# Moving one plane copy ahead of a cast, and two input loads behind two weight loads, in a gated-mix kernel

## The chip, the core and the metric

The kernel runs on one core of a Trainium2 chip. The metric is the device time of one execution in microseconds (us), taken as the median over several runs. The core has five engines that run side by side and wait for each other by semaphores: TensorE (PE, matrix products, with PEld for its weight loads), VectorE (DVE), ScalarE (ACT), GpSimd (POOL) and SyncE (SP, which here only issues DMA transfers). Each engine works through its own instructions in their order.

## The reference

For 2048 tokens of width 512 two branches are computed from one input `x` and mixed by a gate per token:

```
g = sigmoid((x * gate_w).sum(-1))
a = linear attention: q, k, v = x @ wqkv; per head (32 heads of 16)
    phi(t) = [softmax(t @ w_phi), softmax(-t @ w_phi)]
    o = phi_q (phi_k^T v) / (phi_q (phi_k^T 1) + 1e-6);  a = o @ wo
b = experts: q = x @ w_q (32 heads, two halves of 128);
    s1 = q1 @ k1^T, s2 = q2 @ k2^T; the best of 16 in each half names
    one of 256 experts; b = sum over heads of gelu(x . u[e]) * v[e]
out = g * a + (1 - g) * b
```

Two things matter for the change. The scores `s1`, `s2` need products of `w_q` with `k1`, `k2`; the kernel makes these "score weights" once, from 16 pieces `wq0` to `wq15` of 1 MB each, while the attention's keys and values are accumulated. And every token tile of `x` is needed as a pair of a high and a low part.

## The kernel before

The tokens are cut into 16 tiles of 128. A first phase (about the first 120 us) computes keys and values for all tiles, accumulates `phi_k^T v`, and builds the score weights. A second phase runs tile by tile over queries, scores, softmax and output. The order of instructions on every engine is the order in which the program writes them (a manual schedule); only semaphore waits move them in time.

The first phase handles tiles 0 to 4 one by one, and then tiles in pairs (5,6), (7,8), ... in the loop `for t in range(5, NT - 1, 2)`. A pair shares products in a Strassen-like way: `Sums.add` forms sums and differences of the two tiles on POOL, in place in their raw buffers, and `Sums.high` and `Sums.low` split them into high and low parts. The products of a pair are written as PE groups named by their PSUM banks: `pk` (keys), `pe`, `pu`, `pv`.

Loads of `x`: `x_load(t)` gives tile `t` one of four raw buffers (tag `xr`) and issues a 256 KB DMA on SP's queue. `x_high` casts it on ACT (L152), `x_low` subtracts on DVE (L156). In the pass for pair (5,6) the list `more` holds tiles 9 and 10, the second pair behind the one at work.

Score weights: two pieces of `wq` go through PE into one PSUM bank `ws` (`score_w`, L299), and each piece's buffer is then refilled by `load_wq` on SP's queue (L143). Since `ws` comes out in the wrong orientation, it is turned by a DMA transpose on 16-bit planes. `score_planes(j)` copies `ws` to the plane tile `wpl` on ACT (L304) and issues the transpose into `wtp` on SP's queue (L306). A later "join" puts the planes together: `join_tp` copies `wtp` to the f32 tile `wtj` on ACT (L315), and `join_end` casts `wtj` to the high part `sh` on ACT (L321) and subtracts the low part `sl` on POOL (L322). `wpl`, `wtp` and `wtj` have one buffer each, so that a plane copy waits for the transpose before it, a transpose for the join copy before it, and a join copy for the POOL subtraction before it. In the pass t = 5 there are two joins: the one of `ws1` and, after `score_planes(2)` (the score weights made in the pass of tile 4), the one of `ws2`. `score(1)` twice then makes `ws3` and calls `score_planes(3)`.

`k_diffs`, `k_exp`, `k_sum`, `k_mult` are the softmax of one tile's keys: DVE (L115 to L121), ACT (L267), DVE (L271, L272), POOL (L276).

Of the kernel before, what the change touches and what calls it, by code (L numbers as in the profile page):

```python
# [9 lines left out]
F32 = mybir.dt.float32  # L10
# [10 lines left out]
P = 128  # L21
S = 2048
D = 512
NT = S // P
# [11 lines left out]
def mix_kernel(ctx, tc, xT, wqT, wkT, wv, wphi, wo, wq, kk, ug, ev, cst, out):  # L36
# [6 lines left out]
    def mm_bank(name):  # L43
        return psum.tile([P, 512], F32, tag="mm", bufs=4, name=name)

    def tr_bank(name):
        return psum.tile([P, 512], F32, tag="tr", bufs=3, name=name)
# [24 lines left out]
    def x_parts(i, first):  # L72
        xt[i, first] = x_part(i, first)
# [59 lines left out]
    wa_ = ca.enter_context(tc_pool("wl", "left"))  # L133
# [6 lines left out]
    def stage(src, name, shape=None):  # L140
        t_ = wa_.tile(shape or [P, NK, D], F32, tag="st", bufs=2, name=name)
        if src is not None:
            sp.dma_start(t_, src)  # L143
        return t_

    def x_load(t):
        r = rawx[t] = wa_.tile([P, NK, P], F32, tag="xr", bufs=4, name=f"xr{t}")
        if t > 0:
            sp.dma_start(r, xT[t])

    def x_high(t, ks=slice(0, NK)):
        (dve.tensor_copy if t < 3 else act.copy)(x_of(t)[0][:, ks], rawx[t][:, ks])  # L152

    def x_low(t, ks=slice(0, NK)):
        h, l = x_of(t)
        dve.tensor_tensor(l[:, ks], rawx[t][:, ks], h[:, ks], op=ALU.subtract)  # L156

    def x_split(t, ks=slice(0, NK)):
        x_high(t, ks)
        x_low(t, ks)  # L160
# [80 lines left out]
    phis, vs, pks, wsP, stk, joins = {}, {}, {}, {}, {}, []  # L241

    def v_tile(t):
        v = vs[t] = home(t).tile([P, H, F + 1], F32, name=f"v{t}", tag="v")
        if t < NT - 1:
            pool.memset(v[:, :, F], 1.0)
        return v[:, :, :F]
# [9 lines left out]
    def k_diffs(t):  # L257
        phis[t] = home(t).tile([P, 1024], F32, tag="d", name=f"d{t}")
        stk[t] = w1.tile([P, 192], F32, tag="stt", name=f"st{t}")
        softmax_diffs(pks.pop(t), phis[t], stk[t])  # L260
# [5 lines left out]
    def k_exp(t):  # L266
        act.activation(phis[t], phis[t], AF.Exp)  # L267

    def k_sum(t):
        d, st = phis[t], stk[t]  # L270
        dve.tensor_reduce(st[:, 64:128], g64(d), axis=AX.X, op=ALU.add)  # L271
        dve.reciprocal(st[:, 128:192], st[:, 64:128])  # L272

    def k_mult(t):
        d, st = phis[t], stk.pop(t)
        pool.tensor_tensor(g64(d), g64(d), b64(st[:, 128:192]), op=ALU.mult)  # L276

    def kvacc(t):
        n = F + 1 if t < NT - 1 else F
        for g in range(8):  # L280
            for c in range(4):
                h = 4 * g + c
                pe.matmul(acc[32 * c:32 * c + 32, g, :n], phis[t][:, 32 * h:32 * h + 32],
                          vs[t][:, h, :n], start=(t == 0 and g == 0),
                          stop=(t == NT - 1), skip_group_check=True)
# [8 lines left out]
    def score_w(i, raw):  # L294
        j, par = i // 2, i % 2
        if par == 0:
            wsP[j] = tr_bank(f"ws{j}")
        for c in range(4):
            pe.matmul(wsP[j][32 * c:32 * c + 32, :], kp[:, j // 4, par, :], raw[:, c, :],  # L299
                      start=(par == 0), stop=(par == 1))  # L300

    def score_planes(j):
        pl = wa_.tile([P, 2, D], U16, tag="wpl", bufs=1, name=f"wpl{j}")
        act.copy(pl, wsP.pop(j).bitcast(U16).rearrange("p (c j) -> p j c", j=2))  # L304
        tp = wa_.tile([P, 8, P], U16, tag="wtp", bufs=1, name=f"wtp{j}")
        sp.dma_start_transpose(tp, pl.rearrange("p j c -> p (j c)"))  # L306
        joins.append((j, tp))
# [6 lines left out]
    def join_tp(j, tp, tj):  # L314
        act.copy(tj.bitcast(U16).rearrange("p (k n j) -> p j k n", j=2, n=P),  # L315
                 tp.rearrange("p (j k) n -> p j k n", j=2))

    def join_end(j, tj):
        js = slice(P * j, P * j + P)
        t3 = tj.rearrange("p (k e) -> p k e", k=NK)  # L320
        act.copy(sh[:, :, js], t3)  # L321
        pool.tensor_tensor(sl[:, :, js], t3, sh[:, :, js], op=ALU.subtract)  # L322
# [56 lines left out]
    def load_wq():  # L379
        if len(raws) < 16:  # L380
            raws.append(stage(wq[len(raws)], f"wq{len(raws)}"))
# [11 lines left out]
    def spare(src, name, shape):  # L393
        t_ = wa_.tile(shape, F32, tag="xr", bufs=4, name=name)
        sp.dma_start(t_, src)
        return t_
# [3 lines left out]
    def score(n, planes=True):  # L400
        nonlocal done
        for _ in range(n):
            score_w(done, raws[done])
            done += 1
            load_wq()
            if planes and done % 2 == 0:
                score_planes(done // 2 - 1)

    def join_all():
        old = list(joins)  # L410
        joins.clear()
        for j, tp in old:
            score_join(j, tp)
# [39 lines left out]
    def prod(o, left, right, first):  # L453
        for i, ((ah, al), (bh, bl)) in enumerate(zip(left, right)):
            for j, (x_, w_) in enumerate(((ah, bh), (ah, bl), (al, bh))):
                pe.matmul(o, x_, w_, start=(first and i + j == 0), stop=(i == 1 and j == 2),  # L456
                          skip_group_check=True)
# [8 lines left out]
    for t in range(5, NT - 1, 2):  # L466
        n = t + 1
        more = [u for u in (t + 4, t + 5) if u < NT]
        for u in more:
            x_load(u)  # L470
        if t == NT - 5:
            rawu = [spare(ug[:, 0:2], "rawu0", [P, 2, NU])]
        elif t == NT - 3:
            rawu.append(spare(ug[:, 2:4], "rawu1", [P, 2, NU]))
            rawe = [spare(ev[:, 0], "rawe0", [P, D])]
        for u in (t + 2, t + 3):
            if u < NT - 1:
                x_low(u)
        if behind:
            k_diffs(behind)  # L480
        a = pks[t] = mm_bank(f"pk{t}")
        prod(a, tile_of(t, 0), b11, True)
        b = mm_bank(f"pu{t}")
        act.copy(b, a)
        if t + 3 < NT:
            Sums.add(t + 2)
        if t < NT - 3:
            join_all()
        else:
            (j6, tp), = joins  # L490
            joins.clear()
            tj6 = wa_.tile([P, D], F32, tag="wtj", bufs=1, name="wtj6")
            join_tp(j6, tp, tj6)
        e = tr_bank(f"pe{t}")
        prod(e, sums(0, 2), b1, True)
        prod(b, sums(1, 0), b2, False)
        c = mm_bank(f"pv{t}")
        act.copy(c, b)
        if t == 5:
            score_planes(2)  # L500
            k_exp(4)
            k_sum(4)
            k_mult(4)
            join_all()
        prod(a, tile_of(t, 2), b21, False)
        k_diffs(t)
        if behind:
            k_exp(behind)
            k_sum(behind)
            k_mult(behind)  # L510
        score(1)
        if t == NT - 3:
            rawq = stage(wqT, "rawq")
        score(1)
        for u in (t - 3, t - 2):
            kvacc(u)
        vn, vt = v_tile(n), v_tile(t)
        act.copy(vn, by16(e))
        k_exp(t)
        k_sum(t)  # L520
        prod(b, sums(0, 0), b3, False)
        d = pks[n] = mm_bank(f"pk{n}")
        act.copy(d, b)
        prod(c, sums(1, 2), b22, False)
        if t == NT - 3:
            x_split(NT - 1)
        dve.tensor_tensor(vt, by16(c), vn, op=ALU.add)
        dve.tensor_tensor(vn, by16(b), vn, op=ALU.add)
        o2 = d.rearrange("p (c n) -> p c n", c=2)
        prod(o2, tile_of(n, 2), b4, False)  # L530
        if t + 3 < NT:
            Sums.high(t + 2)
            Sums.low(t + 2)
        if t == 7:
            for i in range(2):
                x_parts(i, 11)
        for u in more if n < NT - 4 else ():
            x_high(u)
        k_mult(t)
        behind = n  # L540
    t = NT - 1
# [583 lines left out]
```

## Time and profile before

| what | value |
|---|---|
| time, median of 3 runs | 379.39 us (377.92, 379.39, 380.75) |
| time of the profiled execution | 380.27 us |
| its span, first to last instruction | 378.4 us |
| busy: PE, DVE, ACT, POOL | 97%, 88%, 67%, 54% |
| mean granted clock of TensorE | 0.99 |
| DMA read from and written to main memory | 26.43 MB, 4.19 MB |

The profiled execution lies 1.87 us above its own span (380.27 against 378.4): that is work outside the first and last instruction. TensorE is busy nearly everywhere; the few places where it is idle or runs on a reduced clock lie in the first 120 us, which is also where the change is. Shares over the whole span say little about it; the stretch from 47 to 75 us has to be read by itself.

### The profile page before, as it was taken

The numbers are of one execution on the slowest core, as the hardware profiler recorded it, in microseconds if no ns is written. First come the engines' busy times: TensorE is split into PE (matmuls) and PEld (weight loads), VectorE is DVE, ScalarE is ACT, GpSimd is POOL, SyncE is SP. The second block draws the span as 40 slices with busy tenths as digits, with TensorE's granted clock in tenths as the row PEclk, the third lists the DMA queues.
The fourth block names the chain that finished last, engine by engine and source line by source line (L and its number), as shares of the span: only waits on it lengthen the run. The fifth ranks groups of instructions, "written<-read, shape, count | busy, mean of one in ns | idle before, by whom it ended". The sixth has DMA issues, their size and how long they took to land.

```text
span 378.4 us, 8980 instructions
## 1 busy us (share of the span) xinstructions
PE 368.9 (97%) x3519; PEld 289.7 (77%) x3519; DVE 334.0 (88%) x783; ACT 252.6 (67%) x449; POOL 204.4 (54%) x205
## 2 busy tenths in 40 slices
PE   8999996999999999999999999999999999999996
PEld 4766764778668888878878888888888888888775
DVE  4679885898978889999999999999999999999993
ACT  5576656757756444879668677696686686687741
POOL 1189987498658627636427335344454464364700
PEclk9999996999999999999999999999999999999999
DMA  7867796289665031462341452443523523523201
GB/s 277 332 226 238 232 325 201 94 216 269 248 144 126 3 86 57 84 99 69 86 97 46 108 81 63 84 100 31 122 59 68 125 56 72 127 50 78 65 34 55
DMA packets 72218, 46.67 MB, mean 123 GB/s; under 512 B 63600, under 2 KB 64496, under 8 KB 69872
## 3 DMA queue, kind: packets, MB, share of 16 engines
q1 hardware_dynamic: 71312, 45.24, 45.7%
q10 hardware_dynamic: 864, 0.87, 0.8%
q8 instruction: 27, 0.44, 0.5%
q14 instruction: 15, 0.12, 0.1%
HBM read 26.43 MB, written 4.19 MB: 81 GB/s over the span
## 4 chain that ended last, share of the span: by engine, by line
PE 77%; POOL 8%; DMA 5%; ACT 4%; DVE 3%; issue 2%; ACTq 0%; POOLq 0%; DVEq 0%
PE po L850 11%; PE s L56 8%; PE s L57 8%; PE s L58 8%; PE po L857 5%; PE pq L56 5%; PE pq L58 4%; PE pq L57 4%; PE pk L456 3%; PE oT L738 3%; DMA wtp<-wpl 2%; PE pp L57 2%; PE pp L58 2%; PE pp L56 2%; POOL d L276 2%
## 5 line engine op out<-in xcount | busy, mean ns | idle before, releaser
L652 POOL TENSOR_TENSOR w<-d,zb 128x512 f32<-128x512 f32 x32 | 41.1, 1301 | 78.1 <-ACT d L646 78.1
L56 PE MATMUL s<-sh,xh 128*128 128x512 f32 x128 | 50.9, 398 | 0.0
L57 PE MATMUL s<-sl,xh 128*128 128x512 f32 x128 | 49.9, 390 | 0.0
L58 PE MATMUL s<-sh,xl 128*128 128x512 f32 x128 | 49.9, 389 | 0.0
L687 POOL TENSOR_TENSOR d<-d,st 128x512 f32<-128x512 f32 x30 | 31.2, 1061 | 27.8 <-DVE st L681 25.6
L646 ACT ACTIVATE d<-d 128x512 f32<-128x512 f32 x32 | 20.1, 632 | 35.0 <-DVE d L119 26.9
L276 POOL TENSOR_TENSOR d<-d,st 128x1024 f32<-128x1024 f32 x16 | 33.9, 2118 | 16.0 <-ACT d L267 9.2
L729 ACT COPY pt<-tp 128x1024 uint16<-128x1024 uint16 x28 | 36.3, 1366 | 0.0
L719 ACT COPY pl<-d 128x1024 uint16<-128x1024 uint16 x28 | 29.2, 1044 | 6.9 <-POOL d L687 6.9
L58 PEld LDWEIGHTS s<-sh,xl 128*128 128x128 f32 x128 | 24.0, 188 | 5.1
L56 PEld LDWEIGHTS s<-sh,xh 128*128 128x128 f32 x128 | 24.0, 188 | 4.7
L57 PEld LDWEIGHTS s<-sl,xh 128*128 128x128 f32 x128 | 24.1, 188 | 4.6
L271 DVE TENSOR_REDUCE st<-d 128x64 f32<-128x1024 f32 x16 | 19.4, 1213 | 8.5 <-ACT d L267 8.3
L56 PE MATMUL pq<-wah,xh 128*128 128x512 f32 x64 | 26.8, 418 | 0.0
L58 PE MATMUL pq<-wah,xl 128*128 128x512 f32 x64 | 25.1, 392 | 0.0
L57 PE MATMUL pq<-wal,xh 128*128 128x512 f32 x64 | 25.0, 390 | 0.0
L656 DVE TENSOR_REDUCE st<-d 128x32 f32<-128x512 f32 x32 | 21.6, 683 | 1.9 <-ACT d L646 0.4
L696 DVE TENSOR_TENSOR eq<-s,mx 128x512 bf16<-128x512 f32 x32 | 22.1, 692 | 1.2
L156 DVE TENSOR_TENSOR xl<-xr,xh 128x512 fp32r<-128x512 f32 (+2 forms) x17 | 20.7, 1240 | 1.7 <-ACT xh L152 1.6
L695 DVE TENSOR_REDUCE mx<-s 128x32 f32<-128x512 f32 x32 | 21.8, 681 | 0.0
L666 DVE TENSOR_REDUCE st<-w 128x32 f32<-128x512 f32 x32 | 20.4, 676 | 0.1
L267 ACT ACTIVATE d<-d 128x1024 f32<-128x1024 f32 x16 | 17.0, 1064 | 3.9 <-DVE d L121 3.9
(253 smaller groups left out, 1121.9 us busy)
## 6 DMA issues: line engine op xcount, KB each, us to landing
wq<-wq SPq DMA_DIRECT2D x16, 1024.0 KB, 5.7
xr<-xT SPq DMA_DIRECT2D x15, 256.0 KB, 5.1
y<-ot SPq DMA_DIRECT2D x15, 256.0 KB, 2.4
rawk<-wkT SPq DMA_DIRECT2D x1, 1024.0 KB, 6.3
rawq<-wqT SPq DMA_DIRECT2D x1, 1024.0 KB, 6.4
rawo<-wo SPq DMA_DIRECT2D x4, 256.0 KB, 3.7
rawu<-ug SPq DMA_DIRECT2D x2, 258.0 KB, 3.2
rawv<-wv ACTq DMA_DIRECT2D x2, 256.0 KB, 4.4
```

Source lines behind the costliest of these rows:

```text
L56: pe.matmul(o, ah, bh, start=(first and i == 0), stop=False)
L57: pe.matmul(o, ah, bl, start=False, stop=False)
L58: pe.matmul(o, al, bh, start=False, stop=(last and i == n - 1))
L276: pool.tensor_tensor(g64(d), g64(d), b64(st[:, 128:192]), op=ALU.mult)
L652: pool.tensor_tensor(hs(e["w"], i), hs(e["ph"], i), hs(zb, i), op=ALU.mult)
L656: dve.tensor_reduce(pair(e["st"][:, 64:128])[:, :, i], hs(e["ph"], i), axis=AX.X, op=ALU.add)
L687: eng.tensor_tensor(g64(d)[:, gs_], g64(d)[:, gs_], r[:, gs_].unsqueeze(2).to_broadcast([P, 32, F]), op=ALU.mult)
L695: dve.tensor_reduce(mx, p3, axis=AX.X, op=ALU.max)
L696: dve.tensor_tensor(e["eq"][:, 512 * half:512 * half + 512].rearrange("p (h f) -> p h f", f=F), p3, mx.unsqueeze(2).to_broadcast([P, H, F] ...
L719: act.copy(pl, e["ph"][:, halves[i]].bitcast(U16).rearrange("p (c j) -> p j c", j=2))
L729: act.copy(p16[:, :, 4 * i:4 * i + 4, :], e["tp"][i].rearrange("p (j g) n -> p j g n", j=2))
L850: pe.matmul(po, a, b, start=(i == 0), stop=False)
```

## The change

In the pass t = 5 alone, `score_planes(2)` moves forward. Instead of standing behind the join of `ws1` and the copy of `pv5`, its plane copy stands between that join's two halves, directly behind `join_tp`. And in the same pass the loads of `x` tiles 9 and 10 no longer open the pass; they are issued after the second `score(1)`, behind the refills `wq8`, `wq9` and the transpose of `ws3`. No instruction is added or removed: ACT keeps 433 rows, SP 128, PE 2058, DVE 735 and POOL 177 in the listing, and on PE, DVE and POOL their order is the same.

```
@@ -466,8 +466,9 @@
     for t in range(5, NT - 1, 2):
         n = t + 1
         more = [u for u in (t + 4, t + 5) if u < NT]
-        for u in more:
-            x_load(u)
+        if t > 5:
+            for u in more:
+                x_load(u)
@@ -484,7 +485,14 @@
-        if t < NT - 3:
+        if t == 5:
+            (j1, tp), = joins
+            joins.clear()
+            tj1 = wa_.tile([P, D], F32, tag="wtj", bufs=1, name="wtj1")
+            join_tp(j1, tp, tj1)
+            score_planes(2)
+            join_end(j1, tj1)
+        elif t < NT - 3:
             join_all()
@@ -497,7 +505,6 @@
         if t == 5:
-            score_planes(2)
             k_exp(4)
@@ -512,6 +519,9 @@
         score(1)
+        if t == 5:
+            for u in more:
+                x_load(u)
         for u in (t - 3, t - 2):
             kvacc(u)
```

ACT in the first half of the pass t = 5. The names are tiles with the tile or join number and a buffer number behind it. Before:

```order
L484 COPY pu5_590<-pk5_583 128x512
L315 COPY wtj1_596<-wtp1_453 128x2x512
L321 CAST sh_71<-wtj1_596 128x4x128
L498 COPY pv5_613<-pu5_590 128x512
L304 COPY wpl2_615<-ws2_532 128x1024
L267 ACTIVATE d4_526<-d4_526 128x1024
L315 COPY wtj2_623<-wtp2_617 128x2x512
```

Now:

```order
L485 COPY pu5_586<-pk5_579 128x512
L315 COPY wtj1_592<-wtp1_453 128x2x512
L304 COPY wpl2_594<-ws2_532 128x1024
L321 CAST sh_71<-wtj1_592 128x4x128
L506 COPY pv5_613<-pu5_586 128x512
L267 ACTIVATE d4_526<-d4_526 128x1024
L315 COPY wtj2_619<-wtp2_596 128x2x512
```

The plane copy `wpl2` has moved up by two instructions; the cast `sh` and the copy `pv5` come one instruction later, and everything from `d4` on keeps its place.

SP's queue over the same pass and the start of the next one. Before:

```order
L143 DMA wq7_543<-wq 128x2048
L149 DMA xr9_577<-xT 128x512
L149 DMA xr10_579<-xT 128x512
L306 DMA_TRANSPOSE wtp2_617<-wpl2_615 128x8x128
L143 DMA wq8_644<-wq 128x2048
L143 DMA wq9_650<-wq 128x2048
L306 DMA_TRANSPOSE wtp3_654<-wpl3_652 128x8x128
L149 DMA xr11_757<-xT 128x512
L149 DMA xr12_759<-xT 128x512
```

Now:

```order
L143 DMA wq7_543<-wq 128x2048
L306 DMA_TRANSPOSE wtp2_596<-wpl2_594 128x8x128
L143 DMA wq8_640<-wq 128x2048
L143 DMA wq9_646<-wq 128x2048
L306 DMA_TRANSPOSE wtp3_650<-wpl3_648 128x8x128
L149 DMA xr9_652<-xT 128x512
L149 DMA xr10_654<-xT 128x512
L149 DMA xr11_757<-xT 128x512
L149 DMA xr12_759<-xT 128x512
```

The two loads `xr9` and `xr10` have moved past two transposes and two 1 MB refills, and now stand directly ahead of `xr11` and `xr12`.

## The prediction

> **What bounds the kernel now.** I read the clock row of the page first, then the chain that ended last, then the stretch from 47 to 75 us engine by engine, and last how long each transfer of that stretch took to land. The change touches only ACT and SP, so ACT's rows come first (start, duration, what; in brackets the idle time before, and its releaser):
>
> ```profile
> 47.34 1.36 ACT L315 COPY wtj<-wtp 128x1024 uint16<-128x1024 uint16 x1
> 48.73 0.62 ACT L321 CAST sh<-wtj 128x512 fp32r<-128x512 f32 x1
> 49.58 0.57 ACT L498 COPY pv<-pu 128x512 f32<-128x512 f32 x1 [0.22 <-PE pu L456]
> 50.06 1.02 ACT L304 COPY wpl<-ws 128x1024 uint16<-128x1024 uint16 x1
> 50.96 1.07 ACT L267 ACTIVATE d<-d 128x1024 f32<-128x1024 f32 x1
> 56.02 1.35 ACT L315 COPY wtj<-wtp 128x1024 uint16<-128x1024 uint16 x1 [3.99 <-POOL sl L322]
> 60.27 0.60 ACT L523 COPY pk<-pu 128x512 f32<-128x512 f32 x1
> 61.82 1.14 ACT L152 CAST xh<-xr 128x512 fp32r<-128x512 f32 x2
> 66.44 0.57 ACT L484 COPY pu<-pk 128x512 f32<-128x512 f32 x1 [3.48 <-PE pk L456]
> ```
>
> ACT stands still for 3.99 us, from 52.03 to 56.02, ahead of the second join copy. From there it works without a gap to the copy `pk` that ends at 60.87, and PE waits for exactly that copy:
>
> ```profile
> 52.70 1.07 PE L299 MATMUL ws<-wq,kp 128*32 128x512 f32 x8 [0.81 <-DMA wq<-wq]
> 57.45 0.39 PE L456 MATMUL pv<-wbh,xl 128*128 128x512 f32 x1
> 60.92 0.79 PE L456 MATMUL pk<-sh,xh 128*128 128x512 f32 x1 [3.08 <-ACT pk L523]
> 67.97 0.39 PE L456 MATMUL pu<-uh,xh 128*128 128x512 f32 x1
> ```
>
> PE loses 3.08 us there, and then more, because the granted clock falls (columns behind the stretch and its length: PE, PEld, DVE, ACT, POOL, clock, DMA share, GB/s):
>
> ```profile
> 57.60:57.90 0.30, 0.24 (x2) 0.00 (x0) 0.00 (x0) 0.30 (x1) 0.29 (x1) 1.00 1.04 437
> 60.00:60.30 0.30, 0.00 (x0) 0.00 (x0) 0.00 (x0) 0.30 (x2) 0.00 (x0) 0.77 0.35 84
> 66.90:67.20 0.30, 0.30 (x2) 0.23 (x2) 0.30 (x2) 0.30 (x2) 0.21 (x1) 0.85 0.00 0
> ```
>
> The clock is 1.00 until about 60.1, 0.50 after that, and full again from about 66.95. The chain gives the price:
>
> ```profile
> 60.92 5.49 PE pk L456 x12
> 66.41 1.72 PE pe L456 x6
> 69.50 1.36 PE pk L456 x6
> 73.81 9.03 DMA wtp<-wpl
> ```
>
> Six such products take 1.36 us at full clock. The twelve at 60.92 took 5.49 instead of 2.72, the next six 1.72 instead of 1.36: 3.1 us lost. So this place costs about 6.2 us in all, 3.1 of idle PE and 3.1 of slow PE. The question is whether the change moves what ends ACT's 3.99 us.
>
> The copy `wtj2` needs two things: the transpose `wtp2`, and the one `wtj` buffer, which POOL's subtraction `sl` of the first join has to leave. POOL and SP (a transfer's row is its issue):
>
> ```profile
> 51.59 0.73 POOL L175 TENSOR_TENSOR xr<-xr 128x256 f32<-128x256 f32 x1 [1.41 <-DVE xl L156]
> 54.70 1.29 POOL L322 TENSOR_TENSOR sl<-wtj,sh 128x512 fp32r<-128x512 f32 x1
> 48.21 1.37 SPq L149 DMA_DIRECT2D xr<-xT  x2
> 51.10 1.24 SPq L306 DMA_TRANSPOSE wtp<-wpl  x1
> wtp<-wpl SPq DMA_TRANSPOSE x1, 3.9
> 58.97 1.24 SPq L306 DMA_TRANSPOSE wtp<-wpl  x1
> 62.81 1.57 SPq L149 DMA_DIRECT2D xr<-xT  x2
> ```
>
> The fifth row is the landing time of the transpose issued at 51.10: it was there at 55.0. POOL's subtraction ended at 55.99, and ACT started 0.03 us later. So POOL sets this wait, and the transpose is 1.0 us early already.
>
> **The change part by part.**
>
> *The plane copy moves up.* It starts where the cast `sh` started, at 48.73, ends near 49.74, and the transpose is issued there instead of at 51.10: 1.4 us earlier. The cast comes about 0.9 us later, near 49.64, and ends near 50.3; its reader, POOL's subtraction, starts at 54.70 behind four sums, so 4.4 us cover it (without them it would cost the 0.9). The copy `pv5` slides from 49.58 to about 50.15, and its products on PE come after 56. The exponential `d4` starts about 0.3 us earlier, since the 0.22 of waiting for `pu` is now filled with work; DVE's sum of `d4` and POOL's product gain nothing from it, because POOL is at its sums and the subtraction until 55.99.
>
> *What the early transpose brings.* Behind `wq7` alone it cannot land later than the 55.0 of before, because `xr9` and `xr10` no longer stand ahead of it and nothing new does. Its earliest by the quickest transpose of the trace (the 3.5 below) is 53.2. Either way `wtj2` still waits for POOL's subtraction. That one stands behind the sums of tiles 7 and 8, which waited for DVE's `xl` (1.41 us idle, first row), and none of these has moved. ACT starts at 56.02 as before: gain 0.0. Bounds: 0, or 1.4 less if the subtraction was not what held ACT.
>
> *The loads of tiles 9 and 10 move down.* They leave SP's queue at 48.21 and come behind the transpose `wtp3`, whose plane copy ACT makes after `wtj2`, unchanged at 57.93 to 58.94. So they are issued after 58.97 plus 1.24, at 60.21 and near 60.55, 12 us later. `wq7` no longer shares the engines with them. Its landing of before:
>
> ```profile
> wq<-wq SPq DMA_DIRECT2D x1, 1024.0 KB, 7.9
> ```
>
> PE waited 0.81 us for it at 52.70. At most that is saved, and it ends in a longer wait of PE for ACT (3.08 becomes up to 3.9), worth 0.0 by itself.
>
> When do the two loads land? The first two rows are loads on quiet engines (issued at 62.81 and next), the third one beside a waiting transpose, the fourth one behind a `wq`; then the transpose itself, quickest and slowest:
>
> ```profile
> xr<-xT SPq DMA_DIRECT2D x1, 256.0 KB, 2.3
> xr<-xT SPq DMA_DIRECT2D x1, 256.0 KB, 2.7
> xr<-xT SPq DMA_DIRECT2D x1, 256.0 KB, 4.8
> xr<-xT SPq DMA_DIRECT2D x1, 256.0 KB, 5.4
> wtp<-wpl SPq DMA_TRANSPOSE x1, 3.5
> wtp<-wpl SPq DMA_TRANSPOSE x1, 9.0
> ```
>
> By 60.2 the `wq` pieces have drained and only `wtp3` is in flight (58.97 plus 3.5, so 62.5), so I take 3.0 to 3.6: tile 9 near 63.3, tile 10 near 64.1; bounds 62.5 (2.3) and 66.0 (5.4). ACT wants tile 9 at 61.82 and stalls about 1.5 us. Behind the two casts it has nothing until 66.44, when PE releases it: the casts then end near 64.8, 1.6 us ahead. With 5.4 they end at 66.6, and `pu` (L484) comes 0.2 us late; PE reads that copy at 67.97, 0.96 us after it was ready at 67.01. So all of it is covered: 0.0. The transpose `wtp3` itself has no new traffic ahead of it.
>
> DVE is the other reader:
>
> ```profile
> 63.48 3.43 DVE L156 TENSOR_TENSOR xl<-xr,xh 128x512 fp32r<-128x512 f32 x2
> L156 DVE TENSOR_TENSOR xl<-xr,xh x2: 1091/1756/2420, 63.5 to 64.5; 128x512 fp32r<-128x512 f32 x2
> 63.97 2.40 POOL L276 TENSOR_TENSOR d<-d,st 128x1024 f32<-128x1024 f32 x1
> 70.96 0.69 DVE L115 TENSOR_REDUCE st<-pk 128x32 f32<-128x512 f32 x1 [1.66 <-PE pk L456]
> 75.31 1.95 POOL L276 TENSOR_TENSOR d<-d,st 128x1024 f32<-128x1024 f32 x1 [3.89 <-ACT d L267]
> ```
>
> The second of the pair took 2.42 us and ended at 66.91, half a microsecond after POOL's product: it was held up by it. If the first now starts near 64 or later, both run after that product, which itself ends a little earlier, and the pair ends at 66.9 to 67.7. DVE's next idle time is 1.66 us, before 70.96, so the up to 0.8 us are covered; uncovered, they would delay the softmax of tile 7 by as much. POOL's sums of tiles 9 and 10 start as much later and have the 3.89 us of idle in the last row behind them.
>
> *The sum.* 0.0 for the transpose, 0.0 for the loads, 0.0 for PE's longer wait: 380.3 us against the profiled execution. That execution lies 0.9 above the median of the runs (379.39), so my time is 379.4.
>
> [...]
>
> **The rivals.**
>
> *The transpose did hold ACT* (faster). The profile calls POOL's spans rough. If the subtraction had ended early and the transpose released ACT, `wtj2` comes up to 1.4 us earlier, PE's idle time falls to 1.7 and the clock may stay up: 1.4 + 3.1 = 4.5 less, 374.9. Against it: a landing 1.0 us before the start, and a start 0.03 us after the subtraction. Chance 0.09.
>
> *The clock stays up* (faster). The runs of before lie 2.83 us apart, close to the 3.1 of the slow stretch, so some may have gone without it. A median without it: 376.3. Against it: PE's idle time does not get shorter. Chance 0.08.
>
> *The clock stays down longer.* PE idles up to 0.8 us more. If the slow stretch of 6.9 us lasts half as long again, 3.4 us at half speed cost 1.7: 381.1. Against it: PE is fully busy from 60.92 on, as before. Chance 0.06.
>
> *The x pair lands late* (slower). From a landing of tile 10 at 66.8, 6.2 us after its issue, ACT's `pu` copy holds up PE. If it took as long as the slowest transpose, 9.0, it lands at 69.6, the copy ends at 70.8 and PE waits 2.8 us; the 3.08 us of before shows that such a gap halves the clock, 3.1 more: 385.3. For it: the loads share the engines with `wtp3`, and ACT, DVE and POOL all stand behind them in order. Against it: no `wq` is ahead of them. Chance 0.11.
>
> **How the numbers follow.** The forecast has 0.66. The range leaves out the first and last rival, 0.20 together: from 376.3 (clock up) to 382.0 (clock down longer, 381.1, and the 0.9 by which an execution can lie above its median). One per cent, about what a measurement of this kernel can tell from no change, is 3.8 us: below 375.6 lies the first rival, above 383.2 the last. Faster 0.09, within 0.80, slower 0.11.
>
> **What would show it.** Right: the transpose is issued near 49.7 and lands by 55; the second `wtj` copy still starts near 56.0, released by POOL `sl` after some 4.3 us; ACT now stalls about 1.5 us before the L152 casts, for the DMA of `xr`; the `pu` copy still waits for PE; PE's gap ahead of `pk` is 3.1 to 3.9 us, with the clock at 0.50 behind it. Wrong: a `wtj2` copy well before 56, a `pu` copy released by the L152 casts, or PE idle near 68.

## The result, and the profile after

In 20 runs of each kernel on the same chip the changed kernel took 379.76 us (378.46 to 381.73), the one before 379.53 (377.50 to 382.24). The ratio is 1.0005, with a 95% interval from 0.9984 to 1.0026: no change that can be measured, as forecast. The profiled execution took 379.06 us, with a span of 377.2. Of the runs further down, one of the twelve executions with the plane copy alone took 514.29 us at a mean clock of 0.656, and the figures of that run leave it out.

In this execution the pass t = 5 begins 0.68 us later than in the one of before (the copy `wtj1` starts at 48.02 instead of 47.34), which lies ahead of everything that the change moves. Times after are to be read with that shift. ACT after the change (start, duration, what; in brackets the idle time before, and its releaser):

```profile
48.02 1.36 ACT L315 COPY wtj<-wtp 128x1024 uint16<-128x1024 uint16 x1
49.24 1.00 ACT L304 COPY wpl<-ws 128x1024 uint16<-128x1024 uint16 x1
50.14 0.63 ACT L321 CAST sh<-wtj 128x512 fp32r<-128x512 f32 x1
51.17 1.06 ACT L267 ACTIVATE d<-d 128x1024 f32<-128x1024 f32 x1
56.72 1.38 ACT L315 COPY wtj<-wtp 128x1024 uint16<-128x1024 uint16 x1 [4.48 <-POOL sl L322]
64.01 1.25 ACT L152 CAST xh<-xr 128x512 fp32r<-128x512 f32 x2 [1.36 <-DMA xr<-xT]
66.28 0.57 ACT L485 COPY pu<-pk 128x512 f32<-128x512 f32 x1 [1.02 <-PE pk L456]
```

The plane copy is the second row now, and the second join copy still starts when POOL's subtraction ends: 56.72, which is 56.02 plus the shift. Its wait grew from 3.99 to 4.48 us, because the work ahead of it ended earlier. The late `x` pair shows as a new wait of 1.36 us before the casts L152; the copy `pu` behind them is still released by PE, 1.02 us after the casts ended. SP's issues and POOL, with the landing time of the first transpose:

```profile
50.27 1.25 SPq L306 DMA_TRANSPOSE wtp<-wpl  x1
wtp<-wpl SPq DMA_TRANSPOSE x1, 4.1
61.02 4.06 SPq L149 DMA_DIRECT2D xr<-xT  x4
52.27 0.73 POOL L175 TENSOR_TENSOR xr<-xr 128x256 f32<-128x256 f32 x1 [1.41 <-DVE xl L156]
55.39 1.29 POOL L322 TENSOR_TENSOR sl<-wtj,sh 128x512 fp32r<-128x512 f32 x1
```

The transpose was issued at 50.27 and was there at 54.4, 2.3 us before the copy that reads it could start: the change bought 1.3 us of a transfer that nobody waited for. PE and DVE:

```profile
53.44 1.06 PE L299 MATMUL ws<-wq,kp 128*32 128x512 f32 x8 [0.87 <-DMA wq<-wq]
61.65 0.50 PE L456 MATMUL pk<-sh,xh 128*128 128x512 f32 x1 [3.04 <-ACT pk L533]
64.66 3.04 DVE L156 TENSOR_TENSOR xl<-xr,xh 128x512 fp32r<-128x512 f32 x2 [0.38 <-ACT xh L152]
70.46 0.69 DVE L115 TENSOR_REDUCE st<-pk 128x32 f32<-128x512 f32 x1 [0.36 <-PE pk L456]
```

PE's gap is 3.04 us, before it was 3.08. DVE's idle time before the keys of tile 7 shrank from 1.66 to 0.36 us. The late pair took little of that: DVE's subtractions for it ended at 67.70, without the shift 0.1 us later than before (67.02 against 66.91). The rest comes from PE, which delivered the keys of tile 7 about 1.2 us sooner (70.46, without the shift 69.78, against 70.96), because its slow stretch was shorter. The only larger difference between the two executions in this stretch is the clock. It fell again, but later and for a shorter time; the twelve products behind the gap took 4.60 us instead of 5.49, and the next six no more than their full-clock time (stretch and length, PE, PEld, DVE, ACT, POOL, clock, DMA share, GB/s; then two rows of the chain):

```profile
61.80:62.10 0.30, 0.30 (x2) 0.26 (x3) 0.30 (x1) 0.30 (x2) 0.00 (x0) 1.00 1.27 226
62.40:62.70 0.30, 0.30 (x2) 0.20 (x2) 0.30 (x1) 0.25 (x1) 0.30 (x1) 0.50 0.65 57
65.70:66.00 0.30, 0.30 (x3) 0.26 (x2) 0.30 (x1) 0.00 (x0) 0.30 (x1) 0.89 0.22 61
61.65 4.60 PE pk L456 x12
66.25 1.38 PE pe L456 x6
```

That is 1.2 us less of slow PE. The two profiled times differ by 1.2 us as well (379.06 against 380.27), but the equal figures are chance. The pass had begun 0.68 us later, so that at the plane copy of `ws4`, in the next pass, 0.5 us of lead was left (72.27 against 72.78), and the transpose that this copy feeds then landed after 7.6 us instead of 9.03:

```profile
72.27 1.01 ACT L304 COPY wpl<-ws 128x1024 uint16<-128x1024 uint16 x1 [1.09 <-PE ws L299]
wtp<-wpl SPq DMA_TRANSPOSE x1, 7.6
80.97 1.38 ACT L315 COPY wtj<-wtp 128x1024 uint16<-128x1024 uint16 x1 [1.33 <-DMA wtp<-wpl]
```

With the plane copy alone the same transpose took at most 10.85 us (issued at 72.65, its join copy started at 83.50), with the loads alone at most 9.41 (72.80 and 82.21). One profile of each kernel can't tie such differences to the change, and over 20 runs the times show none.

### The profile page after: what moved, and what is told of

The parts are those of the page before. It is cut to its first block, busy times and chain, and to the rows that moved or that the text cites. A ratio compares the mean times of both kernels' runs of the same rounds, so it can differ in the third digit from the quotient of the medians.

```text
span 377.2 us, 8980 instructions
## 1 busy us (share of the span) xinstructions
PE 367.1 (97%) x3519; PEld 288.9 (77%) x3519; DVE 332.3 (88%) x783; ACT 253.2 (67%) x449; POOL 204.9 (54%) x205
## 4 chain that ended last, share of the span: by engine, by line
PE 93%; ACT 3%; DMA 1%; DVE 1%; POOL 1%; issue 0%; ACTq 0%; POOLq 0%
PE po L860 11%; PE s L56 8%; PE s L57 8%; PE s L58 8%; PE pk L456 6%; PE po L867 5%; PE pq L56 5%; PE pq L58 4%; PE pq L57 4%; PE ws L299 3%; PE pu L456 3%; PE oT L748 3%; PE kvacc L283 2%; PE pp L57 2%; PE pp L58 2%; PE pp L56 2%
## 5 line engine op out<-in xcount | busy, mean ns | idle before, releaser
L156 DVE TENSOR_TENSOR xl<-xr,xh 128x512 fp32r<-128x512 f32 (+2 forms) x17 | 18.8, 1126 | 1.9 <-ACT xh L152 1.7
```

## The experiments

My theory had three parts: POOL's subtraction holds the second join copy, so the early transpose brings nothing; the late `x` pair is covered; and the gap of PE costs its own length and a slow stretch (3.08 and 3.1 us in the profile of before). The rivals: the transpose did hold ACT; a gain and a loss cancel; the later transposes bound everything anyway. Each ratio is against the kernel before on the same chip: 380.13 us beside the first four runs below, 379.70 beside the last four.

**The two halves of the change, each alone.** The plane copy alone is the changed kernel with the old head of the pass:

```
-        if t > 5:
-            for u in more:
-                x_load(u)
+        for u in more:
+            x_load(u)
...
-        if t == 5:
-            for u in more:
-                x_load(u)
```

> The plane copy moved up, the x loads left where they were. My theory: nothing on the path, 379.5 within 0.5; transpose issued near 49.7 behind the two x loads, second join copy still released by POOL's subtraction. Rival (two effects that cancel: the early copy gains, the late loads lose): 377 to 378.5.

Measured: ratio 0.9984 (0.9958 to 1.0009), 379.89 us. The loads alone are the same edit the other way round, on the kernel before:

> The x loads moved down, the plane copy left where it was. My theory: 379.5 within 0.5; tile 10 lands near 64.5, ACT's casts end before PE releases the next copy. Rival (the late loads cost, hidden in the changed kernel by the gain of the early copy): 380.5 to 382.

Measured: ratio 1.0010 (0.9988 to 1.0033), 380.21 us. Neither half shows an effect by itself. The intervals leave room for a gain of up to 0.4% from the copy and a loss of up to 0.3% from the loads, so that a gain and a loss that cancel would have to be smaller than that; the rows show neither. The second join copy with the plane copy alone, and then with the loads alone, where the casts wait for the pair as well:

```profile
56.09 1.36 ACT L315 COPY wtj<-wtp 128x1024 uint16<-128x1024 uint16 x1 [4.48 <-POOL sl L322]
```

```profile
56.22 1.37 ACT L315 COPY wtj<-wtp 128x1024 uint16<-128x1024 uint16 x1 [3.99 <-POOL sl L322]
64.35 1.26 ACT L152 CAST xh<-xr 128x512 fp32r<-128x512 f32 x2 [2.21 <-DMA xr<-xT]
```

With the loads alone ACT had nothing to spare any more: the copy `pu` followed the casts without idle time, at 65.58. That is one of the prediction's signs of being wrong. It cost PE nothing, since PE read the copy at 66.96, 0.8 us after it was done.

**POOL's sums behind the first subtraction, in the changed kernel.** If POOL holds the copy, then letting the subtraction go first must free it:

```
-        if t + 3 < NT:
+        if t + 3 < NT and t != 5:
             Sums.add(t + 2)
...
             join_end(j1, tj1)
+            Sums.add(t + 2)
```

> The changed kernel, with POOL's four sums of tiles 7 and 8 moved behind the low-part subtraction of the first join, so that the subtraction no longer stands behind them. My theory (POOL's subtraction, not the transpose, ends ACT's wait before the second join copy): the subtraction ends near 52 instead of 56.7, the second join copy starts when the transpose lands, near 54.4 to 54.6, some 2.2 us earlier than in the changed kernel; PE's gap before pk6 falls from 3.0 to about 0.8 us, the clock stays at 1.00, and the whole is 3.5 to 5 us faster than before: 374.5 to 376. Rival A (the transpose held ACT all along, POOL's spans being rough): the copy stays near 56.7 and the time at 379.5. Rival B (the next stage is the bound anyway, the time of the pass is given back at the next transposes): PE's gap closes but the time moves by less than 1 us.

Measured: ratio 0.9992 (0.9962 to 1.0022), 379.80 us. The first half of the expectation came true and the second did not; a time that moves by less than 1 us is what rival B foretold. ACT, POOL and PE:

```profile
54.32 1.37 ACT L315 COPY wtj<-wtp 128x1024 uint16<-128x1024 uint16 x1 [1.23 <-DMA wtp<-wpl]
51.70 1.29 POOL L322 TENSOR_TENSOR sl<-wtj,sh 128x512 fp32r<-128x512 f32 x1 [1.18 <-ACT sh L321]
63.55 1.26 ACT L152 CAST xh<-xr 128x512 fp32r<-128x512 f32 x2 [3.30 <-DMA xr<-xT]
59.23 0.50 PE L456 MATMUL pk<-sh,xh 128*128 128x512 f32 x1 [0.83 <-ACT pk L534]
65.34 0.50 PE L456 MATMUL pu<-uh,xh 128*128 128x512 f32 x1 [1.74 <-ACT pu L485]
70.28 1.01 ACT L304 COPY wpl<-ws 128x1024 uint16<-128x1024 uint16 x1 [1.27 <-PE ws L299]
82.06 1.38 ACT L315 COPY wtj<-wtp 128x1024 uint16<-128x1024 uint16 x1 [4.43 <-DMA wtp<-wpl]
84.63 0.50 PE L456 MATMUL pu<-eh,gh 128*128 128x512 f32 x1 [0.55 <-ACT pv L507]
```

The copy now starts at 54.32, released by the transpose; so it had been POOL. PE's gap fell from 3.04 to 0.83 us, and the clock stayed at 1.00 in this execution. But what stood behind it in the queue came to light: the casts wait 3.30 us for the late pair, and PE 1.74 us for the `pu` copy behind them. I had not counted that the slack which covered the late pair was itself made of PE's gap and its slow clock.

That does not account for the whole loss. At the plane copy of `ws4` this execution was still 2.0 us ahead of the changed kernel's (70.28 against 72.27). The transpose that this copy feeds took 10.66 us, where it had taken 7.6, and the join copy behind it started 1.1 us later than in the changed kernel (82.06 against 80.97); the wait of 0.55 us and another of 0.80 come after it. In this profile the lead was lost at a later transpose, as rival B says. And the clock did not stay up in every run. Five of the twelve had a mean clock of 0.999 or 1.000 and a median of 377.34 us; the other seven, at 0.996 or less, had 380.79. Where it fell in those seven no profile shows.

**The same move in the kernel before** (`Sums.add` behind `join_all()` at t = 5, plane copy and loads where they were):

> The kernel before (late plane copy, x loads ahead), with only POOL's sums moved behind the first join's subtraction. My theory: now the transpose of the second score weights is what ends ACT's wait; it is issued near 51.1 and lands near 55, so the second join copy starts near 55.0: 1.0 us earlier than before, PE's gap 2.1 us, clock uncertain; time 376 to 378.5, that is 1 to 2.5 us slower than the changed kernel with the same move, which is what the early plane copy is worth once POOL is out of the way. Rival (the early plane copy is worth nothing in any case): as fast as the other one, 375.

Measured: ratio 0.9959 (0.9935 to 0.9982), 378.67 us. That is 0.17 us above the expected range, and not slower than the run above, as I had expected it to be: here the pair is early, so that nothing is lost at the casts. The profile shows the copy released by the transpose, after a late issue:

```profile
52.89 1.24 SPq L306 DMA_TRANSPOSE wtp<-wpl  x1
56.56 1.36 ACT L315 COPY wtj<-wtp 128x1024 uint16<-128x1024 uint16 x1 [2.75 <-DMA wtp<-wpl]
```

**Plane copy up, sums behind the subtraction, loads at the head:**

> Plane copy up and POOL's sums behind the first join's subtraction, x loads left at the head of the pass. The run with the late x loads closed PE's gap before pk6 to 0.83 us but then lost 1.74 us at the pu copy, because ACT stood 3.30 us waiting for the x pair. My theory (with the gap closed, the late x pair becomes the next wait): with the loads early ACT has no wait before the x casts, PE's 1.74 us are gone; the transpose is issued near 50.5 and lands near 55, PE's gap is 1 to 2 us and the clock stays up; 376.5 to 378.5, faster than the run with the late loads by 1 to 3 us. Rival (it is the later transposes that bound the stretch after 72 us, whatever the x loads do): 379.5.

Measured: ratio 0.9965 (0.9939 to 0.9990), 379.05 us; 0.55 us above what I expected at most, and not clearly faster than the run with the late loads (the intervals overlap), though with the right rows for the loads: the casts no longer wait. What I missed was that the transpose, issued at 49.91 behind both loads, took 5.4 us:

```profile
49.91 1.31 SPq L306 DMA_TRANSPOSE wtp<-wpl  x1
wtp<-wpl SPq DMA_TRANSPOSE x1, 5.4
60.28 0.50 PE L456 MATMUL pk<-sh,xh 128*128 128x512 f32 x1 [2.06 <-ACT pk L530]
60.28 4.30 PE pk L456 x12
```

PE's gap was 2.06 us and the clock fell all the same: twelve products in 4.30 us. In four of the twelve runs the mean clock stayed at 0.999 or 1.000, and these had a median of 376.53 us; the other eight had 379.17.

**Transpose first, loads directly behind it, refills behind both:**

```
             score_planes(2)
+            for u in more:
+                x_load(u)
             join_end(j1, tj1)
             Sums.add(t + 2)
...
-        if t == 5:
-            for u in more:
-                x_load(u)
```

> As the run before, but with the x loads between the transpose of the second score weights and the two wq refills: transpose first, x loads 1.3 us behind it. My theory: the transpose lands near 54.4, PE's gap is about 0.8 us, the x pair lands near 55 to 57, long before ACT's casts; neither wait is left and the clock stays up: 375.5 to 377.5, the fastest of all. Rival (bound by the later transposes): 379 to 380.

Measured: ratio 0.9913 (0.9883 to 0.9943), 376.36 us: as expected, and the fastest of all, 3.3 us below the runs of before beside it. Against the run with the late loads only their place differs, and that is worth 0.8%, each taken against the kernel before on its own chip. All six runs had a mean clock of 1.000, so much of this can be the clock: the five runs with the late loads that kept it up had 377.34 us. SP, ACT and PE, with the landing of the loads:

```profile
50.23 1.24 SPq L306 DMA_TRANSPOSE wtp<-wpl  x1
51.57 1.00 SPq L149 DMA_DIRECT2D xr<-xT  x2
xr<-xT SPq DMA_DIRECT2D x2, 256.0 KB, 3.4
54.36 1.37 ACT L315 COPY wtj<-wtp 128x1024 uint16<-128x1024 uint16 x1 [2.17 <-DMA wtp<-wpl]
60.18 1.15 ACT L152 CAST xh<-xr 128x512 fp32r<-128x512 f32 x2
62.33 0.57 ACT L485 COPY pu<-pk 128x512 f32<-128x512 f32 x1 [1.00 <-PE pk L456]
59.28 0.50 PE L456 MATMUL pk<-sh,xh 128*128 128x512 f32 x1 [0.82 <-ACT pk L533]
79.75 1.37 ACT L315 COPY wtj<-wtp 128x1024 uint16<-128x1024 uint16 x1 [4.09 <-DMA wtp<-wpl]
```

Both waits are gone. The last row shows what comes next: a later transpose, behind two refills, holds ACT for 4.09 us. This execution was 3.6 us ahead of the changed kernel's at the plane copy of `ws4` (68.68 against 72.27) and 1.2 us ahead at the join copy behind it (79.75 against 80.97), so the rival of the later transposes is right in part: they do not bound everything, but they took two thirds of this lead.

**The pair made later still,** by issuing both loads of the changed kernel three times:

```
             for u in more:
                 x_load(u)
+            for u in more + more:
+                sp.dma_start(rawx[u], xT[u])
```

> The changed kernel, with both x loads issued three times in a row, each waiting for the one before it, so that the pair lands some 5 to 6 us later, near 69.5 instead of 64.5. My theory (late x pair, covered by slack in the changed kernel): ACT's casts end near 70.5, the pu copy starts there instead of 66.3, PE stands some 3 us before pu, the clock may fall again: 382.5 to 385.5. Rival (the x pair is nowhere near the path): 380.

Measured: ratio 1.0171 (1.0130 to 1.0211), 385.61 us, 0.11 above the expected range. This is the slower rival of the prediction, brought about by an edit:

```profile
69.25 1.36 ACT L152 CAST xh<-xr 128x512 fp32r<-128x512 f32 x2 [6.73 <-DMA xr<-xT]
71.15 0.80 PE L456 MATMUL pu<-uh,xh 128*128 128x512 f32 x1 [5.25 <-ACT pu L485]
71.74 0.63 PE L456 MATMUL pu<-ul,xh 128*128 128x512 f32 x1
```

Casts ending 5.3 us later than in the changed kernel (70.61 against 65.26; about 0.9 of it is a pass that began later) come with 5.9 us more time; the products behind PE's gap of 5.25 us start, from the second on, 0.43 us apart (71.74, 72.17, 72.60), as those of the slow stretch before did, against 0.23 at full clock.

**Work in PE's gap.** Eleven products into an unused bank, in the changed kernel:

```
         prod(c, sums(1, 2), b22, False)
+        if t == 5:
+            dum = tr_bank("dum")
+            for _ in range(11):
+                pe.matmul(dum, x_of(5)[0][:, 0], wbh[:, 0], start=True, stop=True)
```

> The changed kernel, with eleven products of 128x512 into an unused bank added on PE in its gap before pk6, some 2.5 us of work that ends before pk6 can start. My theory (the gap halves the clock, and that costs 1.9 us in the changed kernel's profile, 3.1 in the one of before): the clock stays at 1.00, the twelve pk products take 2.72 us instead of 4.60, the pu copy then waits for the x casts, which end near 65.3, so that 1.0 to 1.8 us are saved: 378 to 378.8. Rival (the slow stretch is covered by what waits for the transposes later): 379.5 to 380.

Measured: ratio 0.9967 (0.9952 to 0.9982), 378.24 us, as expected.

```profile
57.71 2.65 PE L538 MATMUL dum<-wbh,xh 128*128 128x512 f32 x11
61.04 0.50 PE L456 MATMUL pk<-sh,xh 128*128 128x512 f32 x1 [0.67 <-ACT pk L533]
61.04 3.01 PE pk L456 x12
```

The clock stayed up, with a mean of 0.998 or more in all twelve runs, and the whole became 0.33%, or 1.3 us, faster than the kernel before; the changed kernel itself, on its own chip, was at 1.0005 (0.9984 to 1.0026). Nothing reads what the products write. Their bank is one of the three that `ws` and `pe` use in turn, so they also shift that turn by one, which by the order of the program can delay later products but not advance them. So the slow clock is paid for in the end time, at least in part.

## Why the prediction was right, point by point

**What holds ACT.** Right. POOL's subtraction released the second join copy in the changed kernel and in both halves, and once it stood ahead of the sums in the changed kernel the copy started 2.4 us earlier (54.32 against 56.72), released by the transpose. The rival that POOL's spans hide an earlier end is out.

**The plane copy.** Issue foretold near 49.7, measured 50.27, which is 49.6 without the shift; landing by 55, measured 54.4. Forecast at 0.0, and no effect was seen: 0.9984 (0.9958 to 1.0009) alone.

**The x pair.** Foretold: ACT stalls about 1.5 us and ends its casts 1.6 us before PE releases `pu`. Measured: 1.36 us, and 1.02 to spare; with the loads alone 2.21 us, and nothing to spare on ACT. DVE's pair was foretold to end at 66.9 to 67.7 and ended at 67.70, which is 67.02 without the shift; its second subtraction did not run after POOL's product, as foretold, but beside it again (2.40 us, its end 0.55 behind POOL's at 67.15), where in the kernel before each of the two at 50.2, with POOL idle, took 0.68. The price of a later pair was 385.3 in the rival, with a landing 9 us after issue; the run with the loads thrice came to 385.6. The sums agree better than their parts: PE waited 5.25 us there and not 2.8, behind a gap of 1.63 us instead of 3.08. What the step did not say is that its cover depends on the gap that bounds the pass. The run with the sums moved in the changed kernel showed that: with the gap closed, PE waited 1.74 us for the same late loads.

**wq7.** I allowed up to 0.81 us for a faster landing without the two loads behind it. The rows show none: PE waited 0.87 us, and 1.02 with the loads alone. The upper end of that bound, and with it a gap of up to 3.9 us, was not reached; it was 3.04.

**The clock.** The 3.1 us priced from one profile was a single case: 1.9 in the changed kernel's, where the clock fell only after PE had started again. The second rival, a clock that stays up, was priced at 3.1 us less, and that did not hold. In four of the changed kernel's 20 runs the mean clock was 0.999 or 1.000, and these took 379.08 to 380.45 us, median 379.77; the other sixteen had 379.83. In the changed kernel the time was no shorter where the clock stayed up by itself, while keeping it up with added products saved 1.3 us. In the kernel before it was shorter: beside the first four runs, six executions with a mean clock of 0.998 or more had a median of 378.16 us and the other 29 had 380.43; beside the last four it was 378.40 for three and 379.95 for twenty. That is 1.6 to 2.3 us, so the rival was overpriced but not empty. Why the changed kernel gained nothing is not settled: profiles with a smaller gap, like the one with the loads thrice (1.63 us at that place), had also lost time in a wait for `wq` near 45 us, so a late PE may both shorten the gap and cost as much, but no run separates the two. The two rows of that profile:

```profile
45.17 1.07 PE L299 MATMUL ws<-wq,kp 128*32 128x512 f32 x8 [0.77 <-DMA wq<-wq]
61.52 0.50 PE L456 MATMUL pk<-sh,xh 128*128 128x512 f32 x1 [1.63 <-ACT pk L535]
```

## What to carry to other kernels

A wait that names two conditions is worth as much as the later one: read when each was met before moving the earlier one, since here a transfer already 1.0 us early was made 2.3 us early for nothing. The slack that hides a later transfer can come from the very stall one wants to remove, so that an edit which costs nothing today takes back part of the gain of the next one (here 1.74 us of waiting on PE, once its gap had gone from 3.04 to 0.83). Where a queue's order is free, try the transfer with the next reader first and bulk refills last: here that order gave the fastest run, 376.36 us. And a lead won at one wait has to be followed to the end, since there a later transpose took 2.4 of 3.6 us back.

## What the runs showed of the hardware

In these profiles the halving of TensorE's clock did not follow the length of PE's gap alone. In the run with the sums moved in the kernel before, PE stood 2.50 us and the clock stayed at 1.00; with the plane copy up and the loads at the head it stood 2.06 us and the clock fell to 0.50, 1.4 us after PE had started again:

```profile
62.50:63.00 0.50, 0.50 (x4) 0.41 (x3) 0.50 (x2) 0.50 (x2) 0.50 (x1) 1.00 0.04 16
```

```profile
62.50:63.00 0.50, 0.50 (x2) 0.40 (x2) 0.50 (x2) 0.00 (x0) 0.50 (x1) 0.50 0.00 0
```

The slow stretch lasted about 3.4 us in the changed kernel (62.3 to 65.7), behind a gap of 3.04 us, and 6.9 in the one before (60.1 to 66.95), with a gap of 3.08. In the kernel before the clock fell while PE still stood, 0.8 us ahead of its next product (60.92); in the changed kernel 0.7 us after PE had started again (61.65). Nor is it the same in every execution of a kernel: of the changed kernel's 20, four had a mean clock of 0.999 or 1.000 and sixteen of 0.990 to 0.995. What decides when the clock falls, and for how long, no run shows.
